# Products of single heads in 64x32 tiles of the array, and the states' reading turned by TensorE

## The chip, the core and the metric

The kernel runs on one core of a Trainium2 chip. A core has five engines with a queue of instructions each: TensorE (matrix products; PE in the profile, its weight loads PEld), VectorE (DVE), ScalarE (ACT), GpSimd (POOL) and SyncE (SP), which here issues all transfers. Operands lie in SBUF, 128 partitions wide; products land in PSUM, eight banks of 512 float32 values in each partition. The metric is device time in microseconds, from the first to the last instruction and what lies around it.

## The reference

Three parts run one after the other. `x` is 4 batches of 8 heads, 512 tokens, 64 values a head; `state` has 32 rows for each head.

```python
scores = scale * x @ state.T            # per head: 512 x 32
xread  = softmax(scores) @ state        # tokens read the states
scores2 = scale * state @ x.T           # per head: 32 x 512
sread  = softmax(scores2) @ x           # states read the tokens
x = concat([xread, sread], axis=2)      # 4 * (512 + 32) rows of 512
h = x @ w_in                            # 512 -> 1024
solu = h * softmax(h)
ln = (solu - mean) / sqrt(var + 1e-6) * g_ln
x = ln @ w_out                          # 1024 -> 512
h = x @ w2_in                           # 512 -> 2048
out = (h * tanh(softplus(h))) @ w2_out  # 2048 -> 512
```

## The kernel before

The 2176 rows are 17 tiles of 128: four of tokens for each batch, and tile 16 with the 128 states' rows of all batches. The weights arrive as float64 and are narrowed on the chip (`narrow`, L42): two long instructions on VectorE for each piece (L53, L55), the scaling on VectorE or ScalarE (L46 or L48) and a third step on either (L50, L52).

The first stage (up to about 230 us of the trace) does the attention and the first expert layer. `xread @ w_in` is computed as attention weights times (state @ w_in), so each batch needs these products:

- Scores (`front_scores`, L304): the states of a pair of heads are the weights, 64 columns with the other head's places zero, over all 128 partitions; the moving operand is the pair's x, 512 columns. Two pairs fill the 128 output rows of one buffer `st` of the pool `ps_m`. Batch 0 has token scores (L315) besides.
- States times w_in (`sw_part`, L439, for batches 0 and 1; `sw_pair`, L451, for two batches at once): the same weights against a half of w_in, 512 columns, split into a high and a low part (`swh`, `swl`; L445, L446, L457, L458).
- The states' reading (`attn_rest`, `attn_back`): exponentials of `st` are turned, so that tokens stand on partitions, either by TensorE (L405) or by VectorE, a transfer to DRAM and four back (L393, L396, L409). The string of flags `V` in the plan says which: three of the eight go by DRAM. Then x, 128 tokens by 128 columns, is loaded as weights, and 64 columns of attention weights move (L417). Each pair's result is used on two quarters and dropped on the others.

`stage_a0` (L488) multiplies attention weights by these state products, `stage_a1` to `stage_a3` do the softmax and the normalisation, `stage_c` and `stage_e` turn the result, by TensorE (L542) or by VectorE and DRAM (L550, L553, L563; flags `Y`), and `stage_d` multiplies by w_out (L584, buffers `pm` of the pool `ps_m`, which has two). The turned tiles and the loads of w2 share three buffers, `w64_p`, in the order in which they ask for them.

The second stage is the last layer, in three passes over the rows (L727 products into 2048, L708 to L710 out of them).

All are float32 products, or float32 split into two parts of a shorter format. What sets the order is `PLAN`, a table of steps (`fs`, `rs`, `bk`, `sp`, ...) that names each call with its batch and half, and strings of flags (`@V=...`) that choose engines; the build then arranges each engine's queue from the calls, which gives the rows shown below.

Of the kernel before, what the change touches and what calls it, by code (L numbers as in the profile page):

```python
# [22 lines left out]
P = 128  # L23
# [38 lines left out]
@G=00000000 @H=00000000 @A=11111111 @B=0101111111111101111111111111 @E=0000 @I=10000111 @L=1111111111111111  # L62
@M=11111111 @N=11001101111011101 @O=0000 @P=11111111111111111 @Q=110110010011010001111011 @R=11111001
@S=11111111 @V=00011100 @W=0000000000100100 @X=11100001 @Y=00001111110111111 @Z=00101111011111101
lb,0 lo,0,1 lw,1,1 lw,3,0 lw,0,0 lx,0 lw,1,0 lw,0,1 wi,3,0 lw,2,1 lw,2,0 wi,2,0 wi,0,0 lw,3,1 lo,0,0 ts,0
wi,1,0 fs,0,0 gn,0,0 lo,1,1 lg lx,1 te,0 wi,1,1 wi,0,1 tn,0 gn,1,1 sa,0 rs,0,0 sp,0,0,1,0 sp,0,0,0,0 fs,0,1
tt,0,0 lo,1,0 rs,0,1 sp,0,0,1,1 fs,1,0 ln,0 sp,1,0,1,1 tt,0,1 wi,2,1 g sp,0,1,0,0 wi,3,1 sp,0,1,1,1
sp,0,1,0,1 gs,1,1 bk,0,0 sp,0,0,0,1 lb,1 sp,0,1,1,0 ss,0,0 ss,0,1 a0,0 a1,0 ln,1 fe,1,0 fn,1,0 a0,1 gn,1,0
a1,1 bk,0,1 a0,2 sp,1,1,0,1 fs,1,1 a2,1 sp,1,0,0,1 a2,0 a3,1 lx,2 fe,1,1 fp,1,0 a1,2 sp,1,0,1,0 sp,1,1,0,0
rs,1,0 gn,0,1 bk,1,0 lt gs,0,0 sp,1,1,1,0 fn,1,1 sp,1,0,0,0 sp,1,1,1,1 a3,0 sa,1 ss,1,1 fp,1,1 fs,2,0 ss,1,0  # L70
c,0 a2,2 a0,3 rs,1,1 fs,2,1 fe,2,0 a0,5 fe,2,1 c,1 gs,1,0 fn,2,1 a0,4 a0,6 bk,1,1 e,1 fp,2,1 e,0 a1,3 a1,4
a0,7 a1,5 sa,2,3 fn,2,0 gs,0,1 d,0,0 a2,3 a2,5 a3,2 a3,3 c,2 s2,1 d,0,1 rs,2,0 s2,3 a2,4 s2,2 fp,2,0 rs,2,1
a3,4 a1,6 c,3 a1,7 s2,0 lx,3 e,2 c,4 e,4 a3,5 a0,9 a0,8 a1,9 a2,6 a2,7 a3,6 a3,7 c,6 c,5 ln,2 e,3 a1,8
# [10 lines left out]
def attn_moe_kernel(ctx, tc, xT, xn, bd, w_in, w_out, g_ln, w2i, w2o, out):  # L84
# [173 lines left out]
    with ph1:  # L258
# [13 lines left out]
        bd_t = m1.tile([P, NPAIR, B, 2 * NS], F32, name="bd_t")  # L272
        xs = m1.tile([P, NPAIR, P], F32, name="xs")
# [36 lines left out]
        def tok_scores(b):  # L310
            ph = ps_h.tile([P, 4, 2, 2, 64], F32, tag="ph", name="ph")
            for p in range(NPAIR):
                slot = b if p % 2 == 0 else b ^ 1
                for c in range(4):
                    nc.tensor.matmul(out=ph[:, c, p // 2, pair_row(b, p % 2), :], lhsT=xT_t[b, p][:, c * P:(c + 1) * P],  # L315
                                     rhs=bd_t[:, p, slot, :], start=True, stop=True)
            toks[b] = ph
# [57 lines left out]
        def attn_rest(b, q):  # L375
# [17 lines left out]
            nc.vector.transpose(out=tt.rearrange("p (a k n) -> p a k n", a=4, n=NS),  # L393
                                in_=e2.rearrange("p (k a t) -> p a k t", a=4, t=32))
            td = dram.tile([4, 32, 4, P], F32, tag="ted", name="ted")
            nc.sync.dma_start(out=td.rearrange("r t a e -> (r t) a e"), in_=tt.rearrange("p (a e) -> p a e", a=4))  # L396
            a2s[b, q] = td

        def attn_back(b, q):
            src = a2s.pop((b, q))  # L400
            a2 = at_w.tile([P, 4, 4, NS], F32, tag="a2", name="a2", bufs=1)
            if eng('V', 2 * b + q, True, False):
                tr = ps_t.tile([P, 4, P], F32, tag="tr", name="tr")
                for k in range(4):
                    nc.tensor.transpose(out=tr[:, k, :], in_=src[:, k * P:(k + 1) * P], identity=ident)  # L405
                nc.scalar.copy(out=a2, in_=tr.rearrange("p k (r n) -> p r k n", n=NS))
            else:
                for a in range(4):
                    nc.sync.dma_start(out=a2.rearrange("p r k n -> p r (k n)")[32 * a:32 * a + 32],  # L409
                                      in_=src[:, :, a, :].rearrange("r c e -> c r e"))  # L410
            sr = ps_m.tile([P, 2, 64], F32, tag="mm", name="sr")
            for j in range(2):
                p = 2 * q + j
                r0 = 64 * pair_row(b, j)
                x_ = xn_t.pop((b, p))
                for k in range(4):
                    nc.tensor.matmul(out=sr[:, j, :], lhsT=x_[:, k, :], rhs=a2[:, r0 // NS:r0 // NS + 2, k, :],  # L417
                                     start=k == 0, stop=k == 3)
            for i in range(2):
                nc.scalar.copy(out=xs[64 * i:64 * i + 64, 2 * q:2 * q + 2, b * NS:(b + 1) * NS],  # L420
                               in_=sr[64 * i:64 * i + 64, :, NS * i:NS * i + NS])

        sw = {}
# [9 lines left out]
        def sw_part(b, q, j, hf):  # L433
# [3 lines left out]
            r0 = 64 * pair_row(b, j)  # L437
            slot = b if p % 2 == 0 else b ^ 1
            nc.tensor.matmul(out=sw_ps[b, q][r0:r0 + 64, hf * 512:(hf + 1) * 512], lhsT=bd_t[:, p, slot, :],  # L439
# [8 lines left out]
        def sw_pair(bp, p):  # L448
# [389 lines left out]
```

## Time and profile before

| | us |
|---|---|
| median of 3 runs | 616.72 |
| lowest, highest | 615.06, 617.54 |
| the profiled execution | 615.23 |
| its span (first to last instruction) | 613.4 |
| TensorE busy | 574.9 (94%) |
| VectorE busy | 411.9 (67%) |
| ScalarE busy | 309.9 (51%) |

The span is 1.8 us shorter than the execution's own time, since it leaves out what lies before the first and after the last instruction. Shares of busy time are means over stages that differ; the profile is best read stage by stage. Matmuls are pipelined, so the time of one instruction is longer than the step from one to the next.

### The profile page before, as it was taken

The numbers are of one execution on the slowest core, as the hardware profiler recorded it, in microseconds if no ns is written. First come the engines' busy times: TensorE is split into PE (matmuls) and PEld (weight loads), VectorE is DVE, ScalarE is ACT, GpSimd is POOL, SyncE is SP. The second block draws the span as 40 slices with busy tenths as digits, with TensorE's granted clock in tenths as the row PEclk, the third lists the DMA queues.
The fourth block names the chain that finished last, engine by engine and source line by source line (L and its number), as shares of the span: only waits on it lengthen the run. The fifth ranks groups of instructions, "written<-read, shape, count | busy, mean of one in ns | idle before, by whom it ended". The sixth has DMA issues, their size and how long they took to land.

```text
span 613.4 us, 8430 instructions
## 1 busy us (share of the span) xinstructions
PE 574.9 (94%) x3108; PEld 500.6 (82%) x3108; DVE 411.9 (67%) x729; ACT 309.9 (51%) x592; POOL 32.3 (5%) x105
## 2 busy tenths in 40 slices
PE   2967999999999968999999999999999999999997
PEld 1426689779889968898998999999999998998886
DVE  4799989989899866778889797333333463343332
ACT  3586755664687554556657666222222353233223
POOL 0001212101221100000000000000000000000000
PEclk9977999999999997999999999999999999999999
DMA  8911533530554467555634766423232345234502
GB/s 340 413 52 36 192 99 93 187 84 26 198 213 142 139 211 266 214 207 206 241 109 164 275 227 230 161 103 138 104 137 104 137 155 190 103 138 147 190 7 86
DMA packets 36136, 99.11 MB, mean 162 GB/s; under 512 B 4096, under 2 KB 15872, under 8 KB 35584
## 3 DMA queue, kind: packets, MB, share of 16 engines
q1 hardware_dynamic: 36096, 98.59, 45.3%
q8 instruction: 24, 0.39, 0.3%
q14 instruction: 16, 0.13, 0.1%
HBM read 72.36 MB, written 26.21 MB: 161 GB/s over the span
## 4 chain that ended last, share of the span: by engine, by line
PE 70%; DMA 10%; DVE 10%; ACT 4%; SPq 2%; issue 2%; POOL 0%; ACTq 0%; DVEq 0%
PE hp L727 23%; PE pm L584 9%; PE po L708 9%; PE po L709 9%; PE po L710 9%; PE ph L488 5%; DMA w<-in_w2o 2%; DMA w<-in_w2i 2%; DMA ln_lo<-td 2%; PE sr L417 1%; SPq L563 1%; DMA td<-tt 1%; DMA xT_t<-in_xT 1%; PE ph L315 1%; DVE tt L550 1%
## 5 line engine op out<-in xcount | busy, mean ns | idle before, releaser
L757 ACT ACTIVATE gh<-c 128x384 fp32r<-128x384 f32 (+1 forms) x96 | 48.7, 507 | 148.4 <-DVE c L748 147.1
L708 PE MATMUL po<-w2ol,gh 128*128 128x512 f32 x272 | 106.8, 393 | 0.8 <-ACT gh L757 0.8
L709 PE MATMUL po<-w2oh,gh 128*128 128x512 f32 x272 | 106.5, 391 | 0.0
L727 PE MATMUL hp<-xo,w2r 128*128 128x384 f32 (+1 forms) x504 | 93.8, 329 | 0.6 <-DVE c L748 0.6
L727 PEld LDWEIGHTS hp<-xo,w2r 128*128 128x128 f32 x504 | 86.4, 188 | 5.7 <-DVE c L748 1.0
L727 PE MATMUL hp<-xo,w2swh 128*128 128x384 f32 (+1 forms) x336 | 82.8, 330 | 2.6 <-ACT w2swh L175 1.8
L584 PE MATMUL pm<-ln_lo,gw_hi 128*128 128x256 f32 (+1 forms) x256 | 77.5, 303 | 7.5 <-DVE ln_lo L565 5.1
L710 PE MATMUL po<-w2oh,gl 128*128 128x512 f32 x272 | 82.5, 392 | 0.0
L584 PE MATMUL pm<-ln_hi,gw_hi 128*128 128x256 f32 (+1 forms) x256 | 75.8, 296 | 0.0
L584 PE MATMUL pm<-ln_hi,gw_lo 128*128 128x256 f32 (+1 forms) x256 | 75.2, 294 | 0.0
L727 PEld LDWEIGHTS hp<-xo,w2swh 128*128 128x128 f32 x336 | 60.6, 188 | 8.3 <-ACT w2swh L175 2.0
L708 PEld LDWEIGHTS po<-w2ol,gh 128*128 128x128 f32 x272 | 51.1, 188 | 10.1 <-ACT gh L757 1.6
L584 PEld LDWEIGHTS pm<-ln_lo,gw_hi 128*128 128x128 f32 x256 | 49.2, 192 | 10.5 <-DVE ln_lo L565 5.4
L709 PEld LDWEIGHTS po<-w2oh,gh 128*128 128x128 f32 x272 | 51.1, 188 | 8.3
L710 PEld LDWEIGHTS po<-w2oh,gl 128*128 128x128 f32 x272 | 50.1, 188 | 7.5
L727 PE MATMUL hp<-xo,w2swl 128*128 128x384 f32 (+1 forms) x168 | 55.1, 329 | 0.0
L748 DVE TENSOR_TENSOR c<-hp,u 128x384 f32<-128x384 f32 (+1 forms) x48 | 25.5, 533 | 42.2 <-PE hp L727 42.2
L748 DVE TENSOR_TENSOR c<-hp,m 128x384 f32<-128x384 f32 (+1 forms) x48 | 25.4, 530 | 38.4 <-PE hp L727 37.3
L584 PEld LDWEIGHTS pm<-ln_hi,gw_hi 128*128 128x128 f32 x256 | 49.1, 192 | 1.0 <-issue 0.7
L584 PEld LDWEIGHTS pm<-ln_hi,gw_lo 128*128 128x128 f32 x256 | 49.3, 193 | 0.2
L53 DVE SCALAR_TENSOR_TENSOR w<-w 128x512 uint32<-128x512 uint32 x32 | 22.0, 688 | 15.1 <-ACT w L50 14.8
L727 PEld LDWEIGHTS hp<-xo,w2swl 128*128 128x128 f32 x168 | 31.5, 188 | 0.2 <-DVE w2swl L176 0.2
(343 smaller groups left out, 920.4 us busy)
## 6 DMA issues: line engine op xcount, KB each, us to landing
w<-in_w2i SPq DMA_DIRECT2D x16, 512.0 KB, 6.5
w<-in_w2o SPq DMA_DIRECT2D x16, 512.0 KB, 4.0
td<-tt SPq DMA_DIRECT2D x12, 512.0 KB, 3.0
ln_lo<-td SPq DMA_DIRECT2D x48, 128.0 KB, 2.9
wo<-in_w_out SPq DMA_DIRECT2D x4, 1024.0 KB, 10.9
wi<-in_w_in SPq DMA_DIRECT2D x8, 512.0 KB, 7.6
xT_t<-in_xT SPq DMA_DIRECT2D x16, 256.0 KB, 4.8
xn_t<-in_xn SPq DMA_DIRECT2D x16, 256.0 KB, 2.9
```

The source lines that it names most:

```text
L53: nc.vector.scalar_tensor_tensor(out=low, in0=high, scalar=3, in1=low, op0=ALU.logical_shift_left, op1=ALU.bitwise_or)
L315: nc.tensor.matmul(out=ph[:, c, p // 2, pair_row(b, p % 2), :], lhsT=xT_t[b, p][:, c * P:(c + 1) * P], rhs=bd_t[:, p, slot, :], start=True ...
L417: nc.tensor.matmul(out=sr[:, j, :], lhsT=x_[:, k, :], rhs=a2[:, r0 // NS:r0 // NS + 2, k, :], start=k == 0, stop=k == 3)
L488: nc.tensor.matmul(out=ph[:, hf * 512:(hf + 1) * 512], lhsT=a_[:, c * P:(c + 1) * P], rhs=w_[:, q, hf * 512:(hf + 1) * 512], start=n == 0, ...
L550: nc.vector.transpose(out=tt.rearrange("p (a k t) -> p a k t", a=4, t=32), in_=ez.rearrange("p (k a c) -> p a k c", a=4, c=32))
L584: nc.tensor.matmul(out=pm[:, :n], lhsT=w_[:, k, m * P:(m + 1) * P], rhs=l_[:, c0:c0 + 4 * len(blk), k, :], start=cnt == 0, stop=cnt == 23)
L708: nc.tensor.matmul(out=po[ps, j], lhsT=gh[:, c], rhs=wl, start=first, stop=False)
L709: nc.tensor.matmul(out=po[ps, j], lhsT=gh[:, c], rhs=wh, start=False, stop=False)
L710: nc.tensor.matmul(out=po[ps, j], lhsT=gl[:, c], rhs=wh, start=False, stop=f == NF - 1)
L727: nc.tensor.matmul(out=r, lhsT=w_[:, 0, k * P:(k + 1) * P], rhs=x_[:, k, :n], start=cnt == 0, stop=cnt == 6 * len(terms) - 1)
L748: nc.vector.tensor_tensor(out=r, in0=y, in1=x, op=ALU.add)
L757: nc.scalar.activation(out=gh, in_=src, func=AF.Mish)
```

## The change

- Batch 0 keeps its 64-column weights. For batches 1 to 3 the states are stored without zeros (`st_t`), and each head is a product of its own: 64 partitions (one head of the pair), 32 output columns. Heads are sorted by parity: the even heads of the four pairs fill the 128 rows of one bank, the odd ones another. So eight products with eight operands go to eight places of the array. That holds for the scores (L313) and for states times w_in (`sw_heads`, L468).
- The states' reading loads attention weights and moves x: 64 weight columns and 128 moving ones for batch 0 (L414), 32 and 64 for the others (L423), the sum of both parities in one buffer `sr`. The result has states on partitions and is turned once more by TensorE (L432).
- All eight turns of the attention weights go by TensorE (L403); the way through DRAM is gone. The engine flags and the order of the plan differ too.

```diff
-            st = ps_m.tile([P, S], F32, tag="mm", name="st")
+            if b == 0:
+                ...
             for j in range(2):
-                p = 2 * q + j
-                r0 = 64 * pair_row(b, j)
-                slot = b if p % 2 == 0 else b ^ 1
-                nc.tensor.matmul(out=st[r0:r0 + 64, :], lhsT=bd_t[:, p, slot, :], rhs=xT_t.pop((b, p)),
-                                 start=True, stop=True)
-            sts[b, q] = st
+                sts[b, j] = ps_m.tile([P, S], F32, tag="mm", name="st")
+            for p in range(NPAIR):
+                x_ = xT_t.pop((b, p))
+                for j in range(2):
+                    nc.tensor.matmul(out=sts[b, j][NS * p:NS * p + NS, :], lhsT=st_t[of_head(j), p, b, :],
+                                     rhs=x_[of_head(j), :], start=True, stop=True)
...
-            if eng('V', 2 * b + q, True, False):
-                a2s[b, q] = e2
-                return
-            tt = f32(w64_p.tile([P, 512, 2], U32, tag="w64", name="et").rearrange("p a b -> p (a b)"))[:, :S]
-            nc.vector.transpose(out=tt.rearrange("p (a k n) -> p a k n", a=4, n=NS),
-            ...
+            a2s[b, q] = e2
...
-            for j in range(2):
-                p = 2 * q + j
-                r0 = 64 * pair_row(b, j)
-                x_ = xn_t.pop((b, p))
+                if q == 0:
+                    srs_t[b] = ps_m.tile([P, P], F32, tag="mm", name="sr")
+                sr = srs_t[b]
                 for k in range(4):
-                    nc.tensor.matmul(out=sr[:, j, :], lhsT=x_[:, k, :], rhs=a2[:, r0 // NS:r0 // NS + 2, k, :],
-                                     start=k == 0, stop=k == 3)
+                    for p in range(NPAIR):
+                        r = slice(NS * p, NS * p + NS)
+                        nc.tensor.matmul(out=sr[r, of_head(q)], lhsT=a2[:, k, r], rhs=xn_t[b, p][:, k, of_head(q)],
+                                         start=k == 0, stop=k == 3)
...
+            srs = at_w.tile([P, P], F32, tag="srs", name="srs", bufs=1)
+            nc.scalar.copy(out=srs, in_=sr)
+            tr = ps_t.tile([P, 4, P], F32, tag="tr", name="tr")[:, 0]
+            nc.tensor.transpose(out=tr, in_=srs, identity=ident)
...
-        def sw_pair(bp, p):
-            ph = ps_h.tile([P, FF1], F32, tag="ph", name="ph")
-            for hf in range(2):
-                nc.tensor.matmul(out=ph[:, hf * 512:(hf + 1) * 512], lhsT=bd_t[:, p, 2 * bp:2 * bp + 2, :],
-                                 rhs=w_in_half[2 * p + hf], start=True, stop=True)
-            ...
+        def sw_heads(b, hf):
+            ph = ps_h.tile([P, 2, 512], F32, tag="ph", name="ph")
+            for p in range(NPAIR):
+                for j in range(2):
+                    nc.tensor.matmul(out=ph[NS * p:NS * p + NS, j, :], lhsT=st_t[of_head(j), p, b, :],
+                                     rhs=w_in_half[2 * p + hf][of_head(j), :], start=True, stop=True)
+            sw_ps[b, hf] = ph
+
+        def sw_heads_split(b, hf):
+            ph = sw_ps.pop((b, hf))
+            hi, lo = (t[:, :, hf * 512:(hf + 1) * 512] for t in sw[b])
+            nc.scalar.copy(out=hi, in_=ph)
+            nc.vector.tensor_tensor(out=lo, in0=ph, in1=f32(hi), op=ALU.subtract)
...
-@M=11111111 @N=11001101111011101 @O=0000 @P=11111111111111111 @Q=110110010011010001111011 @R=11111001
+@M=11111111 @N=00010001111011101 @O=0000 @P=11111111111111111 @Q=010110010010010001110011 @R=11101010
```

The plan moves instructions in all queues. Three places matter below. The first is TensorE's queue where the states of batches 2 and 3 are multiplied. Before (`ph<-w_in_t,bd_t` are those products, `st` scores, `pm` products with w_out, `tr<-ident,e` turned attention weights):

```order
L451 MATMUL ph<-w_in_t,bd_t 128x512 x4
L584 MATMUL pm<-ln_lo,gw_hi 128x256
...
L451 MATMUL ph<-w_in_t,bd_t 128x512 x2
L405 MATMUL tr<-ident,e_1347 128x128 x4
L304 MATMUL st<-xT_t,bd_t 64x512 x2
L451 MATMUL ph<-w_in_t,bd_t 128x512 x2
```

After, at the same place (`sr` is the states' reading, `srs` its sum):

```order
L403 MATMUL tr<-ident,e_1185 128x128 x4
L468 MATMUL ph<-w_in_t,st_t 32x512 x8
L423 MATMUL sr<-xn_t,a_1068 32x64 x9
L468 MATMUL ph<-w_in_t,st_t 32x512 x8
L423 MATMUL sr<-xn_t,a_1068 32x64 x7
L313 MATMUL st<-xT_t,st_t 32x512 x4
L468 MATMUL ph<-w_in_t,st_t 32x512 x8
L423 MATMUL sr<-xn_t,a_1247 32x64 x16
L313 MATMUL st<-xT_t,st_t 32x512 x4
L432 MATMUL tr<-ident,srs 128x128
L468 MATMUL ph<-w_in_t,st_t 32x512 x8
L506 MATMUL ph<-swh,aThi 128x512 x2
```

The state products now stand in groups of eight, close together, with reading and scores between them instead of products with w_out.

The second place is VectorE's queue at the end of the token softmax of batch 0, whose last step is `ex<-ex,sm`. Before (`wo` pieces of w_out, `w_in_t<-wi` narrowed w_in, `gw_lo` w_out times g, split):

```order
L53 SCALAR_TENSOR_TENSOR wo_136<-wo_136 128x1024
L620 TENSOR_SCALAR g_t<-g_t 128x8
L55 SCALAR_TENSOR_TENSOR w_in_t<-wi_135 128x512
L332 TENSOR_SCALAR sm_222<-sm_222 128x32
L53 SCALAR_TENSOR_TENSOR wo_139<-wo_139 128x1024
L55 SCALAR_TENSOR_TENSOR wo_136<-wo_136 128x1024
L470 SCALAR_TENSOR_TENSOR gw_lo<-wo_138,g_t,gw_hi 128x256
L333 RECIPROCAL sm_222<-sm_222 128x32
L470 SCALAR_TENSOR_TENSOR gw_lo<-wo_138,g_t,gw_hi 128x256 x3
L55 SCALAR_TENSOR_TENSOR wo_139<-wo_139 128x1024
L334 TENSOR_TENSOR ex<-ex,sm_222 128x1024
```

After:

```order
L53 SCALAR_TENSOR_TENSOR wi_134<-wi_134 128x512
L488 SCALAR_TENSOR_TENSOR gw_lo<-wo_138,g_t,gw_hi 128x256
L55 SCALAR_TENSOR_TENSOR w_in_t<-wi_135 128x512
L340 RECIPROCAL sm_231<-sm_231 128x32
L488 SCALAR_TENSOR_TENSOR gw_lo<-wo_138,g_t,gw_hi 128x256
L55 SCALAR_TENSOR_TENSOR w_in_t<-wi_134 128x512
L488 SCALAR_TENSOR_TENSOR gw_lo<-wo_138,g_t,gw_hi 128x256 x2
L341 TENSOR_TENSOR ex<-ex,sm_231 128x1024
L53 SCALAR_TENSOR_TENSOR wo_136<-wo_136 128x1024
L53 SCALAR_TENSOR_TENSOR wo_137<-wo_137 128x1024
```

Two pieces of w_out that were narrowed ahead of the multiplication now come behind it.

The third place is SP's queue at the end of the first stage, where transfers to DRAM (`td<-tt`) and back (`ln_lo<-td`) of turned tiles and loads of the last layer's weights (`w`) share the queue. Before:

```order
L553 DMA td<-tt 128x1024 x2
L563 DMA ln_lo<-td 32x4x256 x8
L151 DMA w_2131<-in_w2i 128x1024
L151 DMA w_2137<-in_w2i 128x1024
L553 DMA td<-tt 128x1024
L151 DMA w_2163<-in_w2o 128x1024
L563 DMA ln_lo<-td 32x4x256 x4
L179 DMA k0h<-w2swh 128x1792
```

After (tile 16 is the last one there and is turned by TensorE, L560):

```order
L571 DMA td<-tt 128x1024 x2
L150 DMA w_2276<-in_w2i 128x1024
L150 DMA w_2282<-in_w2i 128x1024
L150 DMA w_2314<-in_w2o 128x1024
L581 DMA ln_lo<-td 32x4x256 x8
L178 DMA k0h<-w2swh 128x1792
```

The last four transfers back, behind a load of w2o, are now eight, and no transfer of a turned tile stands between the loads.

## Rows read from the trace of the kernel before

**Rows 1.** Stages: us; busy us of PE, PEld, DVE, ACT, POOL; clock; DMA share; GB/s.
```profile
12.00:44.00 32.00, 25.05 (x75) 12.19 (x75) 28.11 (x48) 22.01 (x36) 0.80 (x2) 0.90 0.68 267
...
56.00:205.00 149.00, 145.93 (x934) 123.22 (x933) 137.30 (x210) 96.28 (x170) 27.80 (x86) 1.00 0.41 135
205.00:234.00 29.00, 21.51 (x163) 20.58 (x162) 21.97 (x33) 15.73 (x28) 2.42 (x8) 0.96 0.62 196
234.00:613.40 379.40, 373.27 (x1906) 337.21 (x1905) 209.73 (x415) 164.56 (x343) 0.00 (x0) 0.99 0.44 161
```
**Rows 2.** TensorE in order of time: start, us, line, product, shapes, count.
```profile
13.14 1.97 PE L304 MATMUL st<-xT_t,bd_t 128*64 128x512 f32 x2
...
22.44 1.98 PE L304 MATMUL st<-xT_t,bd_t 128*64 128x512 f32 x4
...
67.91 1.94 PE L439 MATMUL ph<-w_in_t,bd_t 128*64 128x512 f32 x8
...
124.33 1.88 PE L451 MATMUL ph<-w_in_t,bd_t 128*128 128x512 f32 x4
```
**Rows 3.** The chain that ended last, 59 to 72 us: start, us, what.
```profile
59.19 0.44 PE tr L405 x4
59.63 1.73 PE sr L417 x16
61.36 1.01 PE st L304 x4
62.37 3.01 PE ph L488 x12
```
**Rows 4.** TensorE by line, to 280 us: busy us, mean ns; idle before, releaser.
```profile
L417 PE MATMUL sr<-a,xn_t 128*128 128x64 f32 x128 | 15.3, 272 | 1.2 <-DMA a<-ted 1.2
```
**Rows 5.** Weight loads of lines 304 and 451: ns min/median/max, first and last start.
```profile
L304 PEld LDWEIGHTS st<-xT_t,bd_t x32: 132/137/231, 13.1 to 126.6; 128*64 128x64 f32 x32
...
L451 PEld LDWEIGHTS ph<-w_in_t,bd_t x16: 186/189/190, 111.1 to 128.6; 128*128 128x128 f32 x16
```
**Rows 6.** VectorE by line, to 260 us: busy us, mean ns; idle before.
```profile
L458 DVE TENSOR_TENSOR swl<-ph,swh 64x1024 fp32r<-64x1024 f32 x8 | 9.7, 1215 | 0.5 <-ACT swh L457 0.4
L527 DVE TENSOR_SCALAR ez<-ez,lnsm 128x1024 f32<-128x1024 f32 x12 | 9.6, 800 | 3.0 <-POOL lnsm L522 3.0
...
L378 DVE TENSOR_REDUCE m<-st 128x1 f32<-128x512 f32 x8 | 5.3, 659 | 1.9 <-PE st L304 1.9
...
L53 DVE SCALAR_TENSOR_TENSOR wo<-wo 128x1024 uint32<-128x1024 uint32 x4 | 4.9, 1223 | 8.9 <-ACT wo L50 8.8
...
L446 DVE TENSOR_TENSOR swl<-ph,swh 128x1024 fp32r<-128x1024 f32 x4 | 4.8, 1200 | 0.0
...
L350 DVE STREAM_TRANSPOSE tt<-st 128x512 f32<-128x512 f32 x6 | 4.2, 699 | 0.0
...
L393 DVE STREAM_TRANSPOSE et<-e 128x512 f32<-128x512 f32 x3 | 2.1, 705 | 0.0
L46 DVE TENSOR_SCALAR wi<-wi 128x512 f32<-128x512 f32 x4 | 1.7, 419 | 0.0
```
**Rows 7.** VectorE in order of time, the token softmax's last multiplication.
```profile
39.58 1.21 DVE L334 TENSOR_TENSOR ex<-ex,sm 128x1024 f32<-128x1024 f32 x1
```
**Rows 8.** SP in order of time, at the end of the first stage.
```profile
224.75 0.33 SPq L151 DMA_DIRECT2D w<-in_w2o  x1
225.17 1.81 SPq L563 DMA_DIRECT2D ln_lo<-td  x4
```
**Rows 9.** TensorE in order of time; in brackets the wait before, and for whom.
```profile
232.92 0.69 PE L584 MATMUL pm<-ln_lo,gw_hi 128*128 128x384 f32 x1 [5.07 <-DVE ln_lo L565]
```
**Rows 10.** Two stretches behind that wait, columns as in the first group.
```profile
233.00:238.80 5.80, 5.80 (x18) 5.80 (x19) 1.68 (x3) 1.23 (x2) 0.00 (x0) 0.50 0.96 355
238.80:250.00 11.20, 11.20 (x64) 11.20 (x64) 9.49 (x20) 5.98 (x11) 0.00 (x0) 1.00 0.35 126
```
**Rows 11.** ScalarE by line, to 260 us, columns as for VectorE.
```profile
L382 ACT ACTIVATE e<-st,m 128x512 f32<-128x512 f32 x8 | 5.5, 685 | 6.6 <-POOL m L379 5.9 <-DVE m L379 0.7
```

More of the change, by code (lines that the diff above doesn't have):

```diff
@@ L80, with attn_moe_kernel @@
+a3,8 bk,3,1 d,3,1 a1,11 fp,3,0 a0,12 a0,13 a2,11 a1,12 c,8 a1,13 a2,13 a3,11 a3,13 d,3,0 ca e,8 a2,12 ps,2
+a0,14 cs e,9 c,11 xu a3,12 a1,14 a2,14 a0,15 xo,0 a3,14 c,12 c,10 d,4,1 xo,3 d,4,0 e,10 e,11 xo,1 a0,16
+a1,15 a1,16 c,13 d,5,0 xo,4 xo,2 a2,15 po,0 xo,5 d,5,1 e,13 a2,16 a3,15 a3,16 c,15 e,15 c,14 e,12 d,6,1
+d,6,0 c,16 xo,6 pi,0 e,14 po,1 e,16 d,7,1 pi,1 d,7,0
 """
 @with_exitstack
-def attn_moe_kernel(ctx, tc, xT, xn, bd, w_in, w_out, g_ln, w2i, w2o, out):
+def attn_moe_kernel(ctx, tc, xT, xn, bd, stT, w_in, w_out, g_ln, w2i, w2o, out):
@@ new lines, in attn_back @@
+            tr = ps_t.tile([P, 4, P], F32, tag="tr", name="tr")
+            for k in range(4):
+                nc.tensor.transpose(out=tr[:, k, :], in_=src[:, k * P:(k + 1) * P], identity=ident)
+            nc.scalar.copy(out=a2, in_=tr)
+            if "xs" not in tl:
+                tl["xs"] = m1.tile([P, NPAIR, P], F32, tag="xs", name="xs")
+            xs = tl["xs"]
+            tok = slice(b * NS, (b + 1) * NS)
+            if b == 0:
+                sr = ps_m.tile([P, P], F32, tag="mm", name="sr")
+                x_ = [xn_t.pop((b, 2 * q + j)) for j in range(2)]
@@ L412, in attn_back @@
-            for j in range(2):
-                p = 2 * q + j
-                r0 = 64 * pair_row(b, j)
-                x_ = xn_t.pop((b, p))
-                for k in range(4):
-                    nc.tensor.matmul(out=sr[:, j, :], lhsT=x_[:, k, :], rhs=a2[:, r0 // NS:r0 // NS + 2, k, :],
-                                     start=k == 0, stop=k == 3)
+                    for j in range(2):
+                        nc.tensor.matmul(out=sr[of_head(j), :], lhsT=a2[:, k, of_head(j)], rhs=x_[j][:, k, :],
+                                         start=k == 0, stop=k == 3)
+            else:
+                if q == 0:
+                    srs_t[b] = ps_m.tile([P, P], F32, tag="mm", name="sr")
+                sr = srs_t[b]
+                for k in range(4):
+                    for p in range(NPAIR):
+                        r = slice(NS * p, NS * p + NS)
+                        nc.tensor.matmul(out=sr[r, of_head(q)], lhsT=a2[:, k, r], rhs=xn_t[b, p][:, k, of_head(q)],
+                                         start=k == 0, stop=k == 3)
+                if q == 0:
+                    return
+                for p in range(NPAIR):
+                    xn_t.pop((b, p))
@@ L423, in attn_moe_kernel @@
+        srs_t = {}
         sw = {}
@@ L809 @@
         x.reshape(B, NPAIR, 2, 4, P, D).transpose(0, 1, 4, 3, 2, 5)).reshape(B, NPAIR, P, 4, P)
-    bd = np.zeros((P, NPAIR, B, 2 * NS), state.dtype)
-    for b in range(B):
-        for h in range(H):
-            p, j = divmod(h, 2)
-            slot = b if p % 2 == 0 else b ^ 1
-            bd[64 * j:64 * j + 64, p, slot, NS * j:NS * j + NS] = state[b, h].T
+    bd = np.zeros((P, NPAIR, 2 * NS), state.dtype)
+    for h in range(H):
+        p, j = divmod(h, 2)
+        bd[64 * j:64 * j + 64, p, NS * j:NS * j + NS] = state[0, h].T
+    stT = np.ascontiguousarray(state.reshape(B, NPAIR, 2, NS, D).transpose(2, 4, 1, 0, 3)).reshape(P, NPAIR, B, NS)
     g_ln = np.ascontiguousarray(moe_g_ln.reshape(8, P).T)
```

98 lines of the change are left out of this document (41 added, 57 removed).

## Prediction

> **What bounds the kernel now.** I read the stages first: four stretches of the span with the busy time of each engine [rows 1]. From 56 to 205 us TensorE is busy 145.9 of 149 us, and VectorE 137.3 of 149: the middle is bound by TensorE, with VectorE close behind, so a gain on one must be matched on the other. After 234 us TensorE is busy 373 of 379 us with work that the change leaves alone, so whatever is won earlier reaches the end. Ahead of 44 us the chip loads and narrows weights: VectorE 28.1 of 32 us, TensorE 25.1 of 32, where a product takes twice as long as later. From 205 to 234 us TensorE stands still for 7.5 us, 5.1 of them in one wait.
>
> Next I read how long the affected products take on TensorE, in its order of time [rows 2]. A float32 product shows as two instructions (halves). Two things are to be seen. First, overlap: early on, one score product alone (x2) takes 1.97 us, and two of them that write different halves of the output rows (x4) take 1.98 us. Products in different column halves of the array run side by side, each with its own moving operand. Second, at the later pace: four state products (x8) in 64-column tiles take 1.94 us and two of the full-width ones (x4) 1.88, so one product is 0.94. On the chain of waits a pair of scores takes 1.01 us, and eight products of the states' reading (x16) 1.73 us, 0.108 us for each half [rows 3]. The reading moves only 64 columns but loads 128 columns of weights each time.
>
> **TensorE, part by part** (at the granted clock of 1.00 that [rows 1] show from 56 to 205 us, which is the 2.4 GHz level).
>
> Scores of batches 1 to 3: before, 12 products in 6 pairs at 1.01 = 6.1 us. After, 24 products of 64x32 tiles. The order doesn't keep the eight of a batch together: 2 and 6 for batch 1, 4 and 4 for batches 2 and 3. Six pieces, each at least as long as one product: 6 x 1.01 = 6.1. Gain 0.
>
> States times w_in: before, batch 1 costs 2 x 1.94 and batches 2 and 3 cost 4 x 1.88 us, together 11.4. After, six groups of eight products, and these stay together. If all eight tiles overlap, a group costs what a pair does, 1.01, together 6.1: gain 5.3. What the rows show is only two moving operands at once on the same partitions; here it is four, and the overlap of the two halves of the contraction isn't shown at all. If two at a time is the limit, a group costs 1.94, together 11.6: a loss of 0.2. If the row halves take turns too, 3.88, together 23.3: a loss of 11.9. I take full overlap, because the pair in [rows 2] shows no extra cost whatever for its second operand. The Trainium skill (TensorE: Matmul & The Clock Gate, "Measured speedup vs the span model") says that small tiles run together for the length of one product and about 4 ns for each further tile. By it a group would cost about 0.97 us, an estimate with the 0.94 us of one product; no run here shows it for eight tiles.
>
> States' reading: before, 8 groups, the x128 of [rows 4], at 1.73 = 13.8 us. After, batch 0 has 16 halves for each of two groups, 64 weight columns each, in pairs of column tiles: 0.9 to 1.7 us a group by half or all of 0.108 a half; I take 0.9, together 1.8. Batches 1 to 3 have 64 halves each, with 32 weight columns. A load of 64 columns shows 137 ns and one of 128 columns 189 [rows 5], so 26 ns for 32 columns. Bounds: 64 x 26 ns = 1.7 us and, if each half costs as before, 64 x 108 ns = 6.9 us a batch. I take 40 ns a half, nearer to the load, as four column tiles can overlap: 2.6 us, three batches 7.8. Together 9.6: gain 4.2 (bounds: loss of 10.3, gain of 6.9).
>
> Added turns: 12 transposes of attention weights, since all eight now go by TensorE, and 5 of the states' sums, at 0.11 us each (0.44 for four in [rows 3]): 1.9 us.
>
> Changes of tile shape: 16 before the second stage's first product, 39 after. The pair's 1.01 us against 0.94 for two full-width halves puts 0.07 us on going in and out. It is inside the 1.01 above; for the eight reading groups it adds 0.6 us. The Trainium skill (TensorEngine Tiling (Array Packing), "Key Properties") says that changing the tiling mode drains the array, which speaks against a change that interleaves three shapes. The trace agrees only in that there is a cost, and it is the 0.07 us named.
>
> TensorE in sum: 0 + 5.3 + 4.2 - 1.9 - 0.6 = 7.0 us less, nearly all between 56 and 205 us.
>
> **VectorE.** Splitting the state products: 8 instructions of 64 partitions at 1.215 and 4 of 128 at 1.200 [rows 6] become 8 of 128, so -4.9 us. Three transposes into the DRAM turn: -2.1. Engine choices: 3 fewer normalisations on VectorE (-2.4, ScalarE has room with 96 of 149 us busy), 3 fewer scalings of w_in (-1.3). Together 10.7 us. So VectorE doesn't become the bound that eats TensorE's 7.0; I add nothing for it in the middle.
>
> **The start.** TensorE can't begin the large products until the token softmax has its last multiplication, at 39.6 us [rows 7]. In the order, VectorE has ahead of it: before, three narrowings of w_out (two long instructions each), a state split, four scalings; after, one narrowing, no split, one scaling. That is 4 x 1.22 + 1.20 + 3 x 0.42 = 7.3 us less. Bounds: 0 (the loads set it) and 7.3. I take 3.0: the DMA share is 0.68 in this stretch and ScalarE is busy 22 of 32 us, so these come next.
>
> **The end of the stage.** At 224.75 us a load of w2o is issued that had waited for a buffer; the transfers that bring the last turned tiles back are queued on SP behind it, from 225.17 [rows 8]. When that tile is ready, at 232.9, TensorE has waited 5.1 us [rows 9]. Right after this wait the granted clock is 0.50, the 1.2 GHz level: 18 products in 5.8 us, 0.32 each, where the next 64 take 11.2 us at 1.00, 0.175 each [rows 10]. That is 2.7 us more. Up to 7.8 us hang on this. After, the last tile is turned by TensorE, without SP, but eight such transfers still stand behind a w2o load, which now needs a buffer of a turned tile and not one of w2i. Bounds 0 and 7.8; I take 3.5.
>
> **New waits.** The scores of a batch now fill both buffers of the pool that the pm products use, and the reading's sum stays in one from its first group to its second. The pair is free when VectorE has transposed and reduced both, 2 x (0.70 + 0.66) = 2.7 us [rows 6], and ScalarE has read the second, 0.7 more [rows 11]: 3.4. Behind them TensorE has 12 large products, 3.0 us on the chain [rows 3]. By these 0.4 us remains each time if VectorE starts at once, 3.4 if it starts only when they end. I take 1.0 for each of three batches: 3.0 us lost. The removed round trip through DRAM frees SP of 15 transfers; TensorE had waited 1.2 us for one [rows 4], too little to count beside this.
>
> **Sum.** 7.0 + 3.0 + 3.5 - 3.0 = 10.5 us less than the profiled execution's 615.2: 604.7. The median of the runs shown is 616.7, 1.5 above that execution, so I forecast 606.
>
> **Rivals.**
> *Two operands at a time.* The state groups cost 1.94, the piece of six scores 0.5 more: TensorE gains 1.0 instead of 7.0, and the sum is 4.5: 612. For it: no row shows more than two operands, and float32 is the widest data. Against it: the second came free.
> *Row halves take turns* (the slower side). A product on 64 of the 128 rows blocks the other half. Then state groups cost 3.88 (loss of 11.9) and the score pieces double (loss of 6.1): -6.1 - 11.9 + 4.2 - 1.9 - 0.6 leaves TensorE with 16.3 us more than before; with 3.0 + 3.5 - 3.0 the kernel loses 12.8: 630. It decides from the point where a group of eight costs 1.01 + 10.5 / 6 = 2.8 us. For it: no row of before has a product on half the rows.
> *The buffers pile up.* The three holdings cost 3 us each instead of 1, and the end keeps its stall: 10.5 - 6.0 - 3.5 = 1.0, which is 616. For it: TensorE and VectorE are both nearly full in the middle, so a wait there isn't caught up. Against it: VectorE has 10.7 us less to do.
>
> **Chances.** Forecast 0.55, two at a time 0.25, pile-up 0.11, turns 0.09. A change of 0.5% (3.1 us) is about what a measurement of this kernel can tell from none. Faster by more: 0.53 + 0.19 + 0.02 = 0.74; within: 0.02 + 0.06 + 0.06 = 0.14; slower: 0.12, of it 0.09 from the turns and 0.03 from a worse pile-up. The range goes from 597 (start and end near their bounds of 7.3 and 7.8 and the reading at its 6.9 would give 595 even with the new waits) to 616, which takes in the second case and half of the third and leaves the turns out.
>
> **What would show it.** In the profile after: eight state products (x16) in about 1.0 us, not 1.9 or 3.9; a batch's reading in about 2 x 1.3 us; the token softmax's last multiplication near 36.6 us instead of 39.6; the wait ahead of the 384-column pm products well under 5 us; VectorE's state splits all on 128 partitions. The forecast is wrong if a group costs 2.8 us or more, if TensorE's idle time between 56 and 205 us grows from 3 us to over 10, or if the stage that follows starts no earlier although TensorE did less.

## The result, and the profile after

The changed kernel takes 610.56 us, the median of 4 runs (610.18 to 611.51), beside 616.49 (615.06 to 617.54) for the kernel before: a ratio of 0.9908, 95% interval [0.9884, 0.9931], 0.9% faster. The forecast was 606.0, with a range of 597 to 616. The profiled execution has a span of 608.4 us instead of 613.4, 5.0 less.

The stages again, by the columns of [rows 1] (us; busy us of PE, PEld, DVE, ACT, POOL; granted clock; DMA share; GB/s), of the changed kernel:

```profile
12.00:44.00 32.00, 21.43 (x78) 10.80 (x79) 26.96 (x45) 23.90 (x40) 0.32 (x1) 0.95 0.67 261
44.00:56.00 12.00, 6.80 (x42) 5.04 (x40) 12.00 (x23) 6.44 (x16) 2.00 (x5) 0.87 0.30 104
56.00:205.00 149.00, 137.85 (x1089) 111.67 (x1090) 129.20 (x206) 95.69 (x163) 29.89 (x83) 0.94 0.38 123
205.00:234.00 29.00, 29.00 (x221) 28.96 (x220) 21.82 (x39) 12.52 (x22) 3.44 (x5) 1.00 0.58 182
234.00:608.40 374.40, 365.77 (x1875) 329.16 (x1873) 209.57 (x418) 162.56 (x340) 0.00 (x0) 1.00 0.45 161
```

Two of these rows matter. At the end of the first stage, 205 to 234 us, TensorE is now busy all 29.0 us, where it stood still for 7.5. In the middle, 56 to 205 us, it is busy 8.1 us less, 137.85 instead of 145.93: its idle time rose from 3.1 to 11.2 us, and the granted clock fell from 1.00 to 0.94.

What the single pieces became, in TensorE's order of time (start, us, line, product, shapes, count; in brackets the wait before), for [rows 2, 3, 9]:

```profile
35.62 1.05 PE L313 MATMUL st<-xT_t,st_t 64*32 64x512 f32 x4
...
72.00 1.09 PE L468 MATMUL ph<-w_in_t,st_t 64*32 64x512 f32 x16 [2.60 <-ACT ph L534]
77.15 1.96 PE L468 MATMUL ph<-w_in_t,st_t 64*32 64x512 f32 x16 [1.79 <-DVE lnsm L533]
81.51 0.66 PE L423 MATMUL sr<-xn_t,a 128*32 128x64 f32 x32
...
108.25 1.09 PE L468 MATMUL ph<-w_in_t,st_t 64*32 64x512 f32 x16
...
114.90 1.96 PE L468 MATMUL ph<-w_in_t,st_t 64*32 64x512 f32 x16 [2.60 <-DVE swl L476]
...
227.82 0.34 PE L602 MATMUL pm<-ln_lo,gw_hi 128*128 128x384 f32 x1
```

Eight state products take 1.09 us, hardly more than one (0.94). A reading group of 32 halves takes 0.66. The last row is the plainest account of the whole change: the first pm product of 384 columns starts at 227.82 us without a wait. Before, TensorE came to the same product, behind the same 672 pm products of 256 columns and 12 of the next stage, at 227.85 and waited until 232.92 [rows 9]. From this product to the end of the span both take the same, 380.5 and 380.6 us.

That TensorE comes to it at the same time hides two differences. The 528th of those 672 products starts at 205.12 us before and at 207.29 after; behind it both kernels have the same products left up to the one of 384 columns, and the changed one the eight turns of the last tile besides. And the kernel before has two more waits on this way, 0.58 and 1.84 us, that the changed one hasn't (TensorE, three rows before, one after):

```profile
205.12 0.28 PE L584 MATMUL pm<-ln_hi,gw_lo 128*128 128x256 f32 x1
220.38 0.39 PE L584 MATMUL pm<-ln_lo,gw_hi 128*128 128x256 f32 x1 [0.58 <-ACT raw_d L590]
225.38 0.96 PE L727 MATMUL hp<-xo,w2swh 128*128 128x384 f32 x4 [1.84 <-ACT w2swh L175]
```
```profile
207.29 0.28 PE L602 MATMUL pm<-ln_hi,gw_lo 128*128 128x256 f32 x1
```

So ahead of this point the changed kernel is 2.2 us late, and from there to the product of 384 columns it gains 7.3 (20.5 us instead of 27.8): all that was won was won at the end of the stage. Each of these times is of one execution, and the runs of one kernel differ by 1.3 to 2.5 us, so that 2.2 says no more than that the middle brought nothing.

Of [rows 4 to 7], in the order TensorE by line, weight loads, VectorE by line, VectorE in order of time:

```profile
L423 PE MATMUL sr<-xn_t,a 128*32 128x64 f32 x192 | 4.6, 238 | 0.1
```
```profile
L423 PEld LDWEIGHTS sr<-xn_t,a x192: 106/110/177, 81.5 to 157.2; 128*32 128x32 f32 x192
```
```profile
L476 DVE TENSOR_TENSOR swl<-ph,swh 128x1024 fp32r<-128x1024 f32 x6 | 7.3, 1210 | 0.2 <-ACT swh L475 0.2
L462 DVE TENSOR_TENSOR swl<-ph,swh 128x1024 fp32r<-128x1024 f32 x2 | 2.4, 1205 | 0.0
```
```profile
33.13 1.22 DVE L341 TENSOR_TENSOR ex<-ex,sm 128x1024 f32<-128x1024 f32 x1
```

Where the middle lost it, in two stretches by the columns of [rows 1], first of the kernel before, then of the changed one:

```profile
56.00:80.00 24.00, 22.77 (x133) 16.57 (x132) 23.01 (x41) 17.90 (x37) 5.44 (x19) 1.00 0.49 154
108.00:125.00 17.00, 16.28 (x108) 13.55 (x107) 15.62 (x23) 10.23 (x15) 2.82 (x9) 1.00 0.51 173
```
```profile
56.00:80.00 24.00, 19.21 (x110) 11.45 (x110) 23.47 (x45) 19.48 (x34) 7.93 (x23) 0.71 0.22 66
108.00:125.00 17.00, 12.77 (x163) 5.40 (x161) 13.32 (x16) 10.28 (x18) 1.90 (x6) 0.90 0.59 196
```

TensorE stands still 4.8 us in the first and 4.2 in the second, where it was 1.2 and 0.7 before, and what it does between the waits runs partly at the lower clock level (77.15 and 114.90 above: 1.96 us at a granted clock of 0.50, instead of 1.09 at 1.00). The chain of waits of the changed kernel (start, us, what) shows what it waited for:

```profile
49.00 1.19 DVE gw_lo L488 x3
...
70.71 1.25 ACT ph L534 x2
...
75.87 1.23 DVE swl L476
...
82.49 5.10 PE ph L506 x21
...
108.50 2.81 DMA ln_lo<-td
...
117.15 4.81 DMA td<-tt
...
123.30 5.32 DMA ln_lo<-td
...
146.46 6.23 DMA w<-in_w2i
...
153.28 0.36 ACT raw_a L608
153.69 3.17 PE pm L602 x24
```

Until 82 us the chain runs through VectorE, ScalarE and GpSimd (VectorE almost alone from 34 to 52 us), then 25 us through TensorE, then through the round trip of turned tiles by DRAM, VectorE and a load of w2i, and it comes back to TensorE only at 153.69, where TensorE itself had waited 1.7 us. From there to 234 us it doesn't stop.

### The profile page after: what moved, and what is told of

Its sections match the earlier page's. It is cut to its first block, busy times and chain, and to the rows that moved or that the text cites. A ratio compares the mean times of both kernels' runs of the same rounds, so it can differ in the third digit from the quotient of the medians.

```text
span 608.4 us, 8794 instructions
## 1 busy us (share of the span) xinstructions
PE 564.9 (93%) x3309; PEld 487.9 (80%) x3309; DVE 403.5 (66%) x733; ACT 306.0 (50%) x584; POOL 36.4 (6%) x100
## 4 chain that ended last, share of the span: by engine, by line
PE 69%; DVE 13%; DMA 9%; ACT 4%; issue 2%; SPq 1%; POOL 1%; ACTq 0%; DVEq 0%; POOLq 0%
PE hp L743 24%; PE pm L602 10%; PE po L724 9%; PE po L726 9%; PE po L725 9%; PE ph L506 4%; DMA w<-in_w2o 3%; DMA k6l<-w2swl 1%; DMA ln_lo<-td 1%; PE ph L322 1%; PE ph L512 1%; DMA w<-in_w2i 1%; DMA xT_t<-in_xT 1%; PE st L304 1%; DMA td<-tt 1%
## 5 line engine op out<-in xcount | busy, mean ns | idle before, releaser
L602 PE MATMUL pm<-ln_lo,gw_hi 128*128 128x256 f32 (+1 forms) x256 | 74.6, 291 | 1.7 <-ACT raw_a L608 1.7
L764 DVE TENSOR_TENSOR u<-hp,u 128x384 f32<-128x384 f32 (+1 forms) x24 | 12.8, 533 | 25.2 <-PE hp L743 25.2
```

Of the source, the lines that this page charges most:

```text
L602: nc.tensor.matmul(out=pm[:, :n], lhsT=w_[:, k, m * P:(m + 1) * P], rhs=l_[:, c0:c0 + 4 * len(blk), k, :], start=cnt == 0, stop=cnt == 23)
L764: nc.vector.tensor_tensor(out=r, in0=y, in1=x, op=ALU.add)
```

## The experiments

Four theories of what the change is worth. **TensorE**: its work sets the middle, so what the change took from it is won there, and the end adds little. **VectorE**: its work sets the middle instead. **Buffers**: the two wide accumulators (ps_h) are held too long. **End**: the wait at the end is all that was won. The letters in the quoted expectations stand in numbers 1 to 5 and 10 to 12 for what each text says; in 6 to 9, A is TensorE, B VectorE and C the buffers. Ratios are to the kernel before, which ran beside each of them.

**1. The states' products twice.**

```
-            for p in range(NPAIR):
-                for j in range(2):
+            for p, j in [(p, j) for _ in range(2) for p in range(NPAIR) for j in range(2)]:
```


> The changed kernel (610.6 us), with each group of eight state products done twice into the same place: six groups, about 1.0 us each at the 2.4 GHz level, 6.1 us more of TensorE; same result. Theory A (VectorE and ScalarE set the pace where these groups stand, at 72 to 80 and 108 to 122 us of the trace, so TensorE has room there): at most 2 us more, 610.6 to 612.6. Rival B (TensorE still sets the pace of the stage, and the missing gain is somewhere else): 6 us more, 616 to 617.


Measured: 623.06 us, 1.0136 [1.0095, 1.0177], 12.5 us above the changed kernel; neither theory had that. The order of every queue had changed with the edit, since the list scheduler arranges all of them anew.

**2. and 3. The last tile's turn, alone.** In the changed kernel back through DRAM, and in the kernel before by TensorE: one flag each (Y, last place). In the second the last tile's operands take their slot ahead of half the products of the tile that had it, so those products use the last tile's rows; their number is the same.

```
changed kernel:  - @Y=00001111111111110   + @Y=00001111111111111
kernel before:   - @Y=00001111110111111   + @Y=00001111110111110
```


> The changed kernel with one flag back: the last tile is turned by VectorE and DRAM again, as before the change. Theory A (the stall of 5.1 us and the slow clock behind it at the end of the first stage went because this tile no longer goes by DRAM, and that is more than the whole gain of 5.9 us): 5 to 8 us more, 615.5 to 618.5. Rival B (the stall went because the stage is earlier as a whole or because the queue of transfers is ordered in another way): at most 1.5 us more.

> The kernel before (616.5 us), with one flag changed: the last tile is turned by TensorE. Theory A (the stall of 5.1 us and the slow clock behind it hang on this tile's way through DRAM alone): 5 to 8 us less, 608.5 to 611.5. Rival B (another tile of the same block is late as well, and the stall stays in part): at most 3 us less, 613.5 to 616.5.


Measured: the changed kernel without its turn 619.75 us, 1.0058 [1.0032, 1.0084]; the kernel before with it 611.2 us, 0.9915 [0.9892, 0.9939], the ratio of the whole change. The first lies 1.3 us above what was expected, the second inside. This speaks for the end, with the same reserve: both were arranged anew.

**4. and 5. Less VectorE**, in the changed kernel and in the one before.

```
-            mx = sm_p.tile([P, 16], F32, tag="mx", name="mx", bufs=2)
-            nc.vector.reduce_max(out=mx, in_=tt, axis=AX.X)
-            eng('S', ...).tensor_tensor(out=tt, in0=tt, in1=mx..., op=ALU.subtract)
```


> The changed kernel without the maximum and its subtraction in the token softmax of batches 1 to 3 (the exponential takes the scores as they are): 12 instructions and 8.1 us less on VectorE, 2.7 of it for batch 1 between 50 and 66 us. Theory A (VectorE sets the pace from 36 to 82 us and again behind 108): 4 to 8 us less, 602.5 to 606.5. Rival B (the two buffers of ps_m, held by the pair of scores and by the reading, set the pace): within 1.5 us, 609 to 612.

> The kernel before, without the maximum and its subtraction in the token softmax of batches 1 to 3: 8.1 us less on VectorE. Theory A (before the change TensorE set the pace from 56 to 205 us, so that VectorE's time is worth less here than in the changed kernel): 0 to 3 us less, 613.5 to 616.5. Rival B (VectorE set the pace before the change too, and TensorE's products were never the bound of the first stage): 4 to 8 us less, 608.5 to 612.5.


Measured: 614.26 us, 0.9964 [0.9941, 0.9986], and 622.21 us, 1.0118 [1.0070, 1.0167]. Both became slower by leaving work out, outside what either theory expected; a limit doesn't explain that, the new arrangement can. In number 5 the wait at the end grew from 5.1 to 10.5 us.

So from here each engine's queue is chained, instruction by instruction, in the order that it has in the kernel compared with; an added group stands right behind its original. In the traces of 6 to 12 every engine has the order of that kernel, but for the instructions that the edit names. No run holds the order of the changed kernel without an edit; 6, 7, 8 and 10 lie at 609.7 to 611.0, where it lies at 610.56.

**6. The states' products twice, in the same order.**

> The changed kernel with each group of eight products of the states with w_in issued twice (48 more products, 6 groups of about 1.02 us, 6.1 us of TensorE), and with every engine's queue held in the order that it has in the changed kernel, so that nothing else moves. Theory A (TensorE's work is the limit in the middle too, so what the change took from it is what was won): 610.6 + 6.1 = 616 to 618 us. Theory B (VectorE's work from 40 to 84 us sets the first part of the middle, where it is busy all the time while TensorE pauses and falls to half clock): the two groups before 84 us hide, the four after it cost 4.1: 613 to 615.5. Theory C (the two wide ps_h tiles are held too long, by the Square that writes its scratch into them): each group holds one 1 us longer, 616 to 619.


Measured: 609.69 us, 0.9888 [0.9852, 0.9924]; the changed kernel's 0.9908 lies inside, and none of the three theories had that. TensorE did about 5.8 us more, 0.86 for a group at clock 1.00 and 1.49 for the one behind the wait at 77.12 (rows of this run in TensorE's order, among them its first product of 384 columns, then two of its stretches; last, from 12 us to that product, the changed kernel and this run):

```profile
71.98 1.95 PE L468 MATMUL ph<-w_in_t,st_t 64*32 64x512 f32 x32 [2.62 <-ACT ph L534]
77.12 3.45 PE L468 MATMUL ph<-w_in_t,st_t 64*32 64x512 f32 x32 [2.17 <-DVE lnsm L533]
109.24 1.95 PE L468 MATMUL ph<-w_in_t,st_t 64*32 64x512 f32 x32
...
115.94 1.95 PE L468 MATMUL ph<-w_in_t,st_t 64*32 64x512 f32 x32 [1.07 <-DVE swl L476]
...
228.28 0.34 PE L602 MATMUL pm<-ln_lo,gw_hi 128*128 128x384 f32 x1
```
```profile
56.00:80.00 24.00, 19.16 (x137) 10.55 (x137) 23.48 (x45) 18.68 (x33) 7.89 (x23) 0.78 0.22 66
108.00:125.00 17.00, 14.74 (x230) 6.27 (x229) 12.78 (x17) 10.14 (x15) 1.89 (x6) 1.00 0.54 180
```
```profile
12.00:227.82 215.82, 188.90 (x1391) 150.29 (x1392) 188.43 (x308) 138.55 (x239) 35.66 (x93) 0.94 0.43 146
12.00:228.27 216.27, 191.77 (x1487) 150.63 (x1488) 188.00 (x308) 138.49 (x239) 34.97 (x93) 0.96 0.43 146
```

The product of 384 columns comes 0.46 us later than in the changed kernel, not 5.8. Up to it, TensorE's idle time is 2.4 us less (24.50 instead of 26.92), and its busy time only 2.9 us more: about half of the added work went into the pauses, and the rest was made good by the clock. The sixteen products at 115.94 take 1.95 us, as long as the eight at 114.90 in the changed kernel, and the granted clock from 108 to 125 us is 1.00 instead of 0.90. The TensorE theory falls for the changed kernel: its time on the states has no price there. The other two theories had the wrong sizes too, since they let four or all six groups cost. And the 13 us between this run and number 1, the same edit, are the order's.

**7. Without the maximum, in the same order.**

> The changed kernel without the row maximum and its subtraction in the feature softmax of batches 1 to 3 (12 VectorE instructions, 8.1 us, 2.7 of them before 84 us), every queue otherwise in the changed kernel's order. Theory A (TensorE): 609.5 to 611.5. Theory B (VectorE sets 40 to 84 us): 2.7 less there and something of the clock, 606 to 608.5. Theory C (ps_h tiles): 609 to 611.


Measured: 609.80 us, 0.9897 [0.9861, 0.9933]; the product of 384 columns starts at 228.93. Some 8 us less of VectorE's instructions bought nothing; the VectorE theory, which had 606 to 608.5, falls for this part of its work.

**8. The Square's scratch elsewhere, in the same order.**

```
-            nc.scalar.activation(out=ph, in_=ez, func=AF.Square, bias=sz, accum_out=ssq)
+            if "junk" not in tl:
+                tl["junk"] = x2p.tile([P, FF1], F32, tag="x1", name="junk")
+            nc.scalar.activation(out=tl["junk"] if 0 < i < 11 else ph, in_=ez, ...)
```


> The changed kernel with the Square of ten tiles (i = 1 to 10 in the order of processing) writing its unused output to a tile in SBUF instead of back into the ps_h tile, so that this is free about 1.5 to 4 us earlier; every queue in the changed kernel's order. Theory C (the Square's hold on ps_h sets TensorE's waits of 2.6 us at 72.0 and later ones): 606 to 608. Theory A and theory B: the waits move on to the next thing that VectorE owes, 609.5 to 611.5.


One step of the plan (`gs,1,0`) is named earlier besides, since the scratch takes over the buffer that it reads; the queues keep their order.

Measured: 611.02 us, 0.9911 [0.9876, 0.9946]. The wait at 72.0 went, and others came behind it (TensorE's order):

```profile
70.58 1.09 PE L468 MATMUL ph<-w_in_t,st_t 64*32 64x512 f32 x16 [0.20 <-DVE ez L529]
73.57 1.25 PE L562 MATMUL tr<-ident,ez 128*128 128x128 f32 x8 [1.90 <-DVE ln_lo L566]
75.91 1.96 PE L468 MATMUL ph<-w_in_t,st_t 64*32 64x512 f32 x16 [1.08 <-DVE ez L529]
```

The Square's hold by itself is not the cause of the lost time: 2.60 us of wait became 0.20, and 1.90 came 3 us later.

**9. Without gw_lo, in the same order.**

```
-                nc.vector.scalar_tensor_tensor(out=gw_lo[sl], in0=wr[:, k, :], scalar=g_k, ...)
+        nc.gpsimd.memset(f32(gw_lo), 1e-4)
```


> The changed kernel without the 16 VectorE instructions that form gw_lo (L488, 7.5 us, 12 of them or 5.6 us between 40 and 55 us; gw_lo is filled with a constant by GpSimd at the start, its products stay); every queue otherwise in the changed kernel's order. Theory B (VectorE sets 40 to 84 us): what follows comes 5.6 us earlier and TensorE's pauses shrink, 602 to 606. Theory A: 609.5 to 611.5. Theory C: 608 to 610.5.


Measured: 610.05 us over 7 runs (606.84 to 612.94), 0.9907 [0.9870, 0.9945]. The profiled run, the fastest, has the product of 384 columns at 225.11, 2.7 us earlier, with the same pauses (2.65 and 1.98 us); over the runs nothing is left. That VectorE's early work moves the chain by some part of it is possible, more is not shown.

**10. One pair on ScalarE.** The copy to raw_a goes ahead of the narrowing that waits for w2i (153.28 and 152.71 us).

> The changed kernel in its own order but for one pair on ScalarE: the copy of pm to raw_a (L608 at 153.28 us) goes ahead of the narrowing of a loaded w2i (L50 at 152.71 us), which waits for its DMA while TensorE waits 1.7 us for the copy. Theory D (this pair sets when the middle ends, so that all that was saved ahead of it is lost there): the 1.7 us go and what follows starts earlier, 608 to 609.5 us. Theory E (the middle's end is not set there; the gain of the change is the end's): 610 to 611.5.


Measured: 610.68 us over 12 runs (607.77 to 615.68), 0.9929 [0.9899, 0.9959]. TensorE's wait of 1.7 us for raw_a became 0.40 and 0.32; the time didn't move. That the pair sets it is not seen. A part of 1 us isn't ruled out: the runs differ by 7.9 us, and in the profiled one TensorE comes to this place 2.1 us later than in the changed kernel, with a granted clock of 0.73 from 108 to 125 us, where that has 0.90.

**11. The changed kernel's end by DRAM, in the same order.**

The turned tile lies in a buffer of `ez_p` and not of `w64_p`, so that the other tiles and loads keep theirs.

> The changed kernel with its last tile turned through DRAM again as before the change (one VectorE transpose, 5 DMAs, one copy and one subtraction in place of 8 TensorE turns, two copies and two subtractions), all else in the changed kernel's order. Theory E (the change's gain is the wait at the end, 5.1 us, and the slow clock after it): 614.5 to 618 us. Theory M (the gain came from the middle, and the end would fit in anyway): 610 to 612.


Measured: 617.94 us over 12 runs, 1.0048 [1.0017, 1.0078], 7.4 us above the changed kernel (8.6 by the two ratios). The wait is back (profile of the slowest of its runs, 623.28 us, in which TensorE comes to this place 4.6 us later already):

```profile
237.45 0.69 PE L604 MATMUL pm<-ln_lo,gw_hi 128*128 128x384 f32 x1 [5.07 <-DVE ln_lo L585]
```

The end theory holds for the changed kernel: without the turn by TensorE all of its gain is gone.

**12. The kernel before, its end by TensorE, in the same order.** Here the turn stands behind the products that read its slot, so nothing is overwritten early; a buffer of `w64_p` is still taken where the turned tile had one.

```
- c,15 c,16 e,15 ... d,6,0 e,16 d,7,1 d,7,0      @Y=...1
+ c,15 e,15 ... d,6,0 c,16 d,7,1 d,7,0           @Y=...0
```


> The kernel before with nothing changed but its last tile: turned by 8 TensorE transposes, two copies and two subtractions, behind the last products that read the tile's slot, instead of through DRAM; all else in the order of the kernel before. Theory E: the wait of 5.1 us at 227.85 falls to under 1 us, 0.9 us of turns are added, the slow clock behind the wait goes: 609 to 612.5 us, as good as the whole change. Theory M: 614.5 to 617.


Measured: 614.13 us over 12 runs, 0.9986 [0.9959, 1.0012], between what the two theories expected (up to 612.5, and from 614.5): by itself the turn gives little. TensorE's order and VectorE's tell why:

```profile
225.47 0.34 PE L586 MATMUL pm<-ln_lo,gw_hi 128*128 128x384 f32 x1
...
239.18 0.69 PE L586 MATMUL pm<-ln_lo,gw_hi 128*128 128x384 f32 x1 [5.01 <-DVE raw_d L592]
```
```profile
235.83 0.69 DVE L53 SCALAR_TENSOR_TENSOR w<-w 128x512 uint32<-128x512 uint32 x1 [4.78 <-ACT w L50]
...
238.57 0.55 DVE L592 COPY raw_d<-pm 128x384 f32<-128x384 f32 x1
```

The wait for the tile is gone and the products of 384 columns start 7.45 us earlier, at 225.47. Then a wait of 5.01 us takes its place: the copy that frees their buffer stands on VectorE behind the narrowing of a w2o that isn't there yet. In number 3 this copy stands ahead of that narrowing (234.31 and 234.78 us). In the changed kernel it stands on ScalarE, behind a step of such a narrowing too, but behind one only, and it ends before TensorE asks for the buffer, at 236.36:

```profile
234.30 0.68 ACT L50 ACTIVATE w<-w 128x512 uint32<-128x512 uint32 x1 [6.51 <-DMA w<-in_w2o]
234.88 0.48 ACT L608 COPY raw_d<-pm 128x384 f32<-128x384 f32 x1
```
```profile
236.36 0.34 PE L602 MATMUL pm<-ln_lo,gw_hi 128*128 128x384 f32 x1
```

So the gain of the change is two things together: the last tile's turn by TensorE, and queues at the end in which the copy behind the next products comes in time.

## Why the prediction was right and where it was not

The time lies in the range and the direction is right. The sum isn't: 5.0 us of the 10.5 came, and from other terms than those that carried it. Ahead of the end of the stage 7.0 us were to be won (7.0 + 3.0 - 3.0), and the changed kernel is 2.2 us late there; the end was to give 3.5 and gave 7.3. That the time still fell into the range is luck in part: one error made good some of the other.

**Eight tiles at once** (the state groups at 1.01, the scores at no gain): right. 1.09 us for a state group and 1.06 for eight scores at clock 1.00, so both rivals on overlap are out. By the rule of the Trainium skill (TensorE: Matmul & The Clock Gate, "Measured speedup vs the span model"), about 4 ns for each further tile, the estimate was 0.97; this trace has 1.06 to 1.09, and the measurement decides. Of the 11.4 us that the prediction put on the state products before, one piece of 1.94 didn't stand in the middle: 24 of the 32 halves of L439 stand ahead of 38 us.

**The reading**: mis-sized. At clock 1.00 a group of 32 halves takes 0.58 to 0.66 us, 18 to 21 ns a half, where 40 was taken and 26 was the lower bound. That bound is the slope alone between two load times [rows 5], 52 ns for 64 columns; the straight line through both gives 111 ns at 32 columns. A single load in the changed kernel shows 110 ns, and many of them overlap. So TensorE's saving was larger than the 7.0: its busy time from 12 us to the first product of 384 columns fell by 10.9 us, to 188.90, from this in the kernel before:

```profile
12.00:232.91 220.91, 199.79 (x1198) 161.50 (x1197) 198.44 (x311) 140.27 (x243) 31.60 (x98) 0.96 0.46 154
```

**"TensorE in sum 7.0 us less, nearly all between 56 and 205 us"**: this step failed. It took busy time for elapsed time, because TensorE was busy 145.9 of 149 us there. In its place the trace shows 8.1 us more of idle time in the middle and part of the work at the lower clock level, and run 6 shows that in the changed kernel 5.8 us of TensorE's work on the states cost 0.46: there half of it went into pauses that other engines set, and half was made good by the clock. The prediction had named its own sign for this, idle time growing from 3 to over 10 us: it is 11.2. That TensorE's work had no price in the kernel before either is not shown. No run took work from that kernel with its order held, and the new plan, which came with the new products, may have made the waits by itself.

**The start, 3.0**: the last multiplication of the token softmax came 6.5 us earlier than [rows 7], near the bound of 7.3. Behind it TensorE waits 4.4 us at 72.00 and 77.15, and at the 528th product nothing of it is left.

**VectorE adds nothing**: right as far as tried. Some 8 us less of its instructions in 7 and 6.7 in 9 changed no median.

**New waits, 3.0 on the buffers of the pm products**: most came elsewhere. On those buffers TensorE waits 0.46 us for the reading's sum (118.34) and 1.71 for raw_a (153.69) in the middle, 2.2 together, where the kernel before has 1.8 on them. The large ones stand ahead of three state groups (72.00, 77.15, 114.90: 2.60, 1.79 and 2.60, together 7.0), whose operands are long there, so what they wait for is a buffer of ps_h: a term that the prediction put at nothing without a reason. Behind two of them the products run at the lower clock level. It is not one wait that can be taken away: 8 and 10 removed 2.4 and 1.0 us and the time stayed.

**The end, 3.5 of at most 7.8**: mis-sized. All 7.5 us of idle time between 205 us and the product of 384 columns went, the wait of 5.1 and the two of 0.58 and 1.84 that the prediction didn't count. The slow stretch behind it (2.7) went too: from 233 to 238.8 us the clock is 1.00 where [rows 10] have 0.50. But after 234 us TensorE's idle time is 2.5 us more than before, so that nothing is gained behind the product. From the 528th product on that makes 7.3 us, and run 11 prices the term at 7.4. The reserve of the prediction, that transfers still stand behind a w2o load, had no weight: they do, but this load is issued at 210.13 us instead of 224.75, and the last of the eight by 216.8 (SP):

```profile
210.13 0.33 SPq L150 DMA_DIRECT2D w<-in_w2o  x1
213.17 3.65 SPq L581 DMA_DIRECT2D ln_lo<-td  x8
```

Open is what the middle's chain would have to lose for TensorE's saving to show. Four single causes were taken out without a gain that the runs could show (7 to 10); that several chains end close together there is the likely reading, and no run took two out at once. Two pieces of the chain shown above were never tried: the round trip of turned tiles by DRAM (107 to 129 us), and the load of w2i with the buffer that it waits for.

## What to carry to other kernels

A high busy share doesn't price an engine's work: put the saved work back, in the same order, and see whether it costs anything. Look for points that both kernels must pass with the same work behind them, here the 528th product of 256 columns and the first of 384, and compare the time of arrival and the waits apart. And where a scheduler arranges the queues, hold their order before believing an experiment of one or two per cent: the same edit gave 623.06 us with the order free and 609.69 with it held.

## What the hardware showed unexpectedly

Eight tiles of 64x32 with four moving operands on the same 64 rows and two row halves ran in 1.06 to 1.09 us, where one product takes 0.94. A second set of eight behind the first adds 0.86 (6). Weight loads of 32 columns, which show 110 ns each, run so far side by side that 32 loads with their products took 0.58 us. After waits of 1.8 to 2.6 us at 77.15 and 114.90 the state products took 1.96 us at a granted clock of 0.50, the lower level, but the one at 72.00, behind a wait of 2.60, took 1.09 at 1.00; and with more work between the waits (6) the granted clock from 108 to 125 us stayed at 1.00.
